# Sinkhorn-sorted attention and a gated MLP: one load for w_in, earlier loads for the next batch, a new order of units and a new last projection

## The chip, the cores and the metric

The kernel runs on one core of one Trainium2 chip. The metric is the device time of one execution in microseconds (us), the median of several runs. Data lies in device memory (DRAM), on chip in SBUF (128 partitions) and in PSUM, where TensorE's matmuls write. The engines work in parallel and wait for each other by semaphores: TensorE (PE in the profile, its weight loads PEld), VectorE (DVE), ScalarE (ACT), GpSimd (POOL) and SyncE (SP). DMAs are issued by POOL (these convert float32 to bf16 on the way) and by SP; the change adds one by ACT.

## The reference

Two layers follow each other. B = 4 batches, H = 8 heads, S = 768 positions, D = 64; a sequence has 8 blocks of 96 positions.

```python
# attention
P = sort_net                                    # (4, 8, 8, 8)
for _ in range(5):
    P = exp(P - max(P))
    P = P / sum(P, axis=-1)
    P = P / sum(P, axis=-2)
k_sorted = einsum('bhij,bhjcd->bhicd', P, k_b)  # mixes the blocks of a head
v_sorted = einsum('bhij,bhjcd->bhicd', P, v_b)
attn = softmax(q_b @ k_sorted^T / 8)            # inside each block of 96
x = (attn @ v_sorted) as (4, 768, 512)
# gated MLP
h = relu(x @ w_in)                              # 512 -> 1024
u, v = h[..., :512], h[..., 512:]
v_n = (v - mean(v)) / sqrt(var(v) + 1e-6)
v_s = einsum('ts,bsd->btd', w_spatial, v_n) + b_spatial
out = (u * v_s) @ w_out                         # float32 (4, 768, 512)
```

## The kernel before

Work is cut into *units*, each a short burst of matmuls on TensorE into one of four PSUM tiles (two banks each, `ps0` to `ps3`) and the copy, exp or relu that empties the tile. The order of the units, 174 of them, is written out by hand in `SCHEDULE` (lines 518 to 532). Line 538 makes PE, DVE, ACT and POOL follow the order of the program, so a unit's instructions stand on each engine's queue behind those of the unit before. `k10D3` reads: unit `k`, index 1, batch 0, emptied by DVE (`A` for ACT, `-` where the unit fixes it), into `ps3`. A unit can start on PE once its tile is empty and its operands are there.

The units of a batch, with their names in the schedule, are:

- `k` (line 321): the sorted k of two heads, transposed, by 12 matmuls against `pdiag`, the mixing matrix spread out for the layout. `q` (288): the transposed q of four heads, 24 matmuls.
- v comes in one of two ways. In batch 0, `t` (325) and `B` (328) mix and transpose it on PE. In later batches `v` (`vmix`, 261) mixes two heads with 2 matmuls; when both pairs of a half (four heads) are there, SP writes the half to a DRAM scratch `vd` (282) and reads it back as `vb` in another layout (283).
- `s` (`score`, 343): 16 matmuls of 96 x 96 and an exp on ACT into a tile `ex`. `z` (`sums`, 365): the softmax sums, and their reciprocals `lns` by two ACT instructions (375, 376). `a` (`attend`, 379): 32 small matmuls of `ex` with `vb`, four of them side by side in the array, and two DVE products (397) which write a quarter of `xt`, the transposed x.
- `X` and `V` (`vstart`, `vproj`, 427 to 444): the v half of `x @ w_in` in pieces of two row groups, relu on ACT, statistics on DVE. `N` (446) normalizes it. `U` (459): the u half, transposed.
- `S` (`spatial`, 472): `w_spatial` product, 12 matmuls, an add of the bias on DVE (490) and the gate product `gt` on POOL (491; in the last unit of all on DVE). `O` (`oproj`, 494): the product with `w_out`, 8 matmuls, a copy to `o_sb` and the DMA to the output, 512 KB for two row groups.
- `w` (228) transposes w_spatial once.

While the later half of batch b runs, the attention of batch b+1 is woven into it.

x is split so that one half of a head's 64 columns lies in one block of 128 partitions: `attend` takes columns 0 to 31 for `dh` = 0 and 32 to 63 for `dh` = 1 (line 390). The rows of w_in must lie in the same order, so it comes in four DMAs (lines 132 to 140), one for each half of the heads and of the columns.

Loads: `load_heads` (92) brings q, k or v of a batch as one DMA. POOL issues q, k and v of batch 0, w_in, the bias, w_spatial, then v, k and q of batch 1, and w_out; after them it makes `pdiag` of the later batches (547) and `b_bc` (549). The loads of batch b+2 are issued at line 565: after the second unit `S` of batch b, POOL copies two single elements of batch b+1's `vb` into a tile `gate`, which keeps POOL until that batch's v has come back from DRAM, and then issues v, k and q.

In the last batch every `O` unit empties its tile in pieces, DVE and ACT a half row group each, and sends each row group (256 KB) by itself (508 to 512).

Of the kernel before, what the change touches and what calls it, by code (L numbers as in the profile page):

```python
# [8 lines left out]
FP32 = mybir.dt.float32  # L9
BF16 = mybir.dt.bfloat16  # L10
# [6 lines left out]
def _raw_ap(base_ap: bass.AP, off_delta: int, dims) -> bass.AP:  # L17
    return bass.AP(
        tensor=base_ap.tensor,
        offset=base_ap.offset + off_delta,  # L20
        ap=[list(d) for d in dims],
    )
# [8 lines left out]
def kernel(  # L31
# [12 lines left out]
    nc = tc.nc  # L44

    B, H, S, D = q.shape
    NB = sort_net.shape[-1]
    BLK = S // NB
    G = S // 128
    TB = 128 // NB  # L50
    BH = B * H
    DM = H * D
    DFF = moe_w_in.shape[1]
    DH = DFF // 2
    KC = DM // 128
    FC = DH // 128
# [9 lines left out]
    qk_pool = ctx.enter_context(tc.tile_pool(name="qk", bufs=7))  # L66
    ex_pool = ctx.enter_context(tc.tile_pool(name="ex", bufs=8))
    xt_pool = ctx.enter_context(tc.tile_pool(name="xt", bufs=4))
    ln_pool = ctx.enter_context(tc.tile_pool(name="ln", bufs=4))
    moe_pool = ctx.enter_context(tc.tile_pool(name="moe", bufs=4))  # L70
    vs_pool = ctx.enter_context(tc.tile_pool(name="vs", bufs=3))
    vsb_pool = ctx.enter_context(tc.tile_pool(name="vsb", bufs=4))
# [6 lines left out]
    def ps_tile(n, dt=FP32):  # L79
        return psum.tile(  # L80
            [128, 2, 512 if dt == FP32 else 1024], dt, name=f"ps{n}", tag=f"ps{n}",
        )
# [9 lines left out]
    def load_heads(x, b, name):  # L92
        t = ld.tile([128, H, G * D], BF16, name=name, tag=name)
        nc.gpsimd.dma_start(  # L94
            out=t,
            in_=_raw_ap(x, b * H * S * D, [[G * D, 128], [S * D, H], [1, G * D]]),
        )
        return t
# [27 lines left out]
    DQ = D // 2  # L126
# [2 lines left out]

    v_in[0] = load_heads(v, 0, "v_in")  # L130
    w_in_sb = pers.tile([128, KC, DFF], BF16)
    for j in range(2):
        for dh in range(2):
            nc.gpsimd.dma_start(
                out=w_in_sb[:, 2 * j + dh, :],
                in_=_raw_ap(
                    moe_w_in, (j * (H // 2) * D + dh * DQ) * DFF,
                    [[D * DFF, H // 2], [DFF, DQ], [1, DFF]],
                ),
            )  # L140
    nc.gpsimd.dma_start(out=b_nat, in_=_raw_ap(moe_b_spatial, 0, [[0, 128], [1, S]]))
    wsp_nat = pers.tile([128, G, S], BF16)
    nc.gpsimd.dma_start(out=wsp_nat, in_=moe_w_spatial.rearrange("(p g) s -> p g s", g=G))
# [94 lines left out]
    def copy(eng, out, in_):  # L238
        if eng is nc.scalar:
            nc.scalar.copy(out=out, in_=in_)  # L240
        else:
            nc.vector.tensor_copy(out=out, in_=in_)  # L242
# [10 lines left out]
    class Attention:  # L253
# [126 lines left out]
        def attend(self, m, eng, ps):  # L380
            j, ih = m // 2, m % 2
            t = ps_tile(ps)
            for ii in range(NB // 2):
                i = ih * (NB // 2) + ii
                for dh in range(2):
                    for c in range(H // 2):
                        nc.tensor.matmul(  # L387
                            t[c * DQ:(c + 1) * DQ, dh, ii * BLK:(ii + 1) * BLK],
                            lhsT=self.vb[:, i, j, c, dh * DQ:(dh + 1) * DQ],
                            rhs=self.e[4 * j + 2 * (c // 2) + ih][:, c % 2, ii, :],  # L390
                            start=True, stop=True, tile_position=(0, c * DQ),
                        )
            if j not in self.xt:
                self.xt[j] = xts[self.b, j] = xt_pool.tile([128, 2, S], BF16, name="xt", tag="xt")
            i0, r = ih * (NB // 2), self.r[m]
            for dh in range(2):
                nc.vector.tensor_mul(  # L397
                    out=self.xt[j][:, dh, :].rearrange(
                        "p (g i t) -> p i g t", g=G, i=NB)[:, i0:i0 + NB // 2],
                    in0=t[:, dh, 0:HW].rearrange("p (i g t) -> p i g t", g=G, t=TB),  # L400
                    in1=r.rearrange("p (i g t) -> p i g t", g=G, t=TB),
                )


    class Gmlp:
        def __init__(self, b):
            self.b, self.last = b, b == B - 1
            self.v, self.u, self.gt, self.mv = {}, {}, {}, None
            self.vt = {}

        def xt(self, kc):
            return xts[self.b, kc // 2][:, kc % 2, :]
# [79 lines left out]
            self.gt[mc] = gt  # L492

        def oproj(self, n, eng, ps):
            t = ps_tile(ps)
            pairs = [(mc, x) for mc in range(FC) for x in range(2)]
            if self.last and n == G // 2 - 1:
                pairs = [(mc, x) for x in range(2) for mc in range(FC)]
            for mc, x in pairs:
                g = 2 * n + x  # L500
                nc.tensor.matmul(  # L501
                    t[:, x, :], lhsT=self.gt[mc][:, g * 128:(g + 1) * 128],
                    rhs=w_out_sb[:, mc, :],
                    start=(mc == 0), stop=(mc == FC - 1),
                )
            o_sb = o_pool.tile([128, 2, DM], FP32, name="o_sb", tag="o")
            o_dram = out[self.b].rearrange("(p g) n -> p g n", g=G)[:, 2 * n:2 * n + 2, :]
            if self.last:
                for x in range(2):
                    copy(DVE, o_sb[:, x, 0:DM // 2], t[:, x, 0:DM // 2])  # L510
                    copy(ACT, o_sb[:, x, DM // 2:], t[:, x, DM // 2:])
                    nc.sync.dma_start(out=o_dram[:, x, :], in_=o_sb[:, x, :])
            else:
                copy(eng, o_sb, t)
                nc.sync.dma_start(out=o_dram, in_=o_sb)


    SCHEDULE = """
        k00A2 k10D3 k20A0 s10-1 s00-2 s30-3 k30D0 t30D1 t00A2 t20D0 s20-3 s50-1 t10D2 s70-0
        B00D3 s60-1 s40-2 B30D0 B10D3 z00-1 B20D2 z10-0 a00-1 a10-3 z20-2 a20-0 z30-1 a30-2  # L520
        X10-3 X00-1 U20D0 V10-- V00-- w10D2 w30A0 V20-3 v01A1 U10A0 v11A3 v31D2 w00A1 U00D0
        k01A3 v21D1 w40A2 w20D0 w50D3 k11A1 k21A2 k31A0 q11D3 q01D1 N00-- U30A2 s51-0 s71-3
        S10-1 s31-2 s01-0 S20-3 s11-1 s21-2 S00-0 z31-3 z01-1 S30-2 s41-3 s61-0 a01-1 z11-2
        a31-3 a11-0 z21-1 a21-2 O10A3 O00D1 O20D0 V01-2 v32A3 v02D1 V21-0 v22A2 V11-3 v12A0
        U11A1 k32A2 q12D3 k12A0 q02D1 k02D2 N01-- k22A3 U21A0 s32-1 s22-3 S11-2 s72-0 s42-1
        S21-3 s52-2 s02-0 U01A1 s62-3 s12-2 U31D0 z02-1 S01-3 z32-2 z12-1 S31-0 z22-2 a32-3
        a02-1 a22-2 a12-0 O11D3 O01A1 O21A2 V02-0 v33A3 v03D1 V22-2 v23A0 V12-3 v13A2 U12A1
        k33A0 q13D3 k13A2 q03D1 k03D0 N02-- k23A3 U22A2 s33-1 s23-3 S12-0 s73-2 s43-1 S22-3
        s53-0 s03-2 U02A1 s63-3 s13-0 U32D2 z03-1 S02-3 z33-0 z13-1 S32-2 z23-0 a33-3 a03-1
        a23-0 a13-2 O12D3 O02A1 O22A0 V03-2 V13-3 V23-1 N03-- U03A0 U13A2 U23A3 U33A1 S03-0  # L530
        S13-2 S23-3 S33-1 O03A0 O13A2 O23A3
    """
    UNITS = {
        "v": "vmix", "k": "ktr", "q": "qtr", "s": "score", "z": "sums", "a": "attend",
# [3 lines left out]
    with tc.manual_schedule(engines={ET.PE, ET.DVE, ET.Activation, ET.Pool}):  # L538
        attn = {b: Attention(b) for b in range(B)}
        gmlp = {}  # L540
        sinkhorn()
        warm(9, 1)
        attn[0].qtr(0, ACT, 2), attn[0].qtr(1, ACT, 3)
        warm(2, 1)
        transpose_p()
        spread(0, 1, 0), spread(1, 3, 1)
        for x in range(1, B):
            make_pdiag(x, nc.gpsimd, 0, H)
        nc.gpsimd.tensor_copy(
            out=b_bc.rearrange("p (g c) -> p g c", g=G),  # L550
            in_=b_nat.rearrange("p (c g) -> p g c", g=G),
        )
        for step in SCHEDULE.split():
            name, n, b = step[0], int(step[1]), int(step[2])
            eng = {"A": ACT, "D": DVE, "-": None}[step[3]]
            ps = None if step[4] == "-" else int(step[4])
            if name == "w":
                wsp_unit(n, eng, ps)
            elif name in "XVNUSO":
                if b not in gmlp:  # L560
                    gmlp[b] = Gmlp(b)
                if name == "S":
                    eng = DVE if b == B - 1 and len(gmlp[b].gt) == FC - 1 else nc.gpsimd
                getattr(gmlp[b], UNITS[name])(n, eng, ps)
                if name == "S" and b + 2 < B and len(gmlp[b].gt) == 2:
                    gate = small.tile([1, 2], BF16, name="gate", tag="gate")
                    for x in range(2):
                        nc.gpsimd.tensor_copy(
                            out=gate[:, x:x + 1], in_=attn[b + 1].vb[0:1, 0, x, 0, 0:1],
                        )  # L570
                    v_in[b + 2] = load_heads(v, b + 2, "v_in")
                    k_in[b + 2] = load_heads(k, b + 2, "k_in")
                    q_in[b + 2] = load_heads(q, b + 2, "q_in")
            else:
                getattr(attn[b], UNITS[name])(n, eng, ps)


# [28 lines left out]
```

## Time and profile before

| | us |
|---|---|
| median of 8 runs | 166.55 (164.82 to 168.63) |
| the profiled execution, its own time | 165.71 |
| its span in the profile | 163.9 |
| PE busy with matmuls | 145.5 (89% of the span) |
| PE's weight loads | 85.4 |
| DVE busy | 98.7 |
| ACT busy | 92.2 |
| POOL busy | 50.4 |
| DMA traffic | 23.89 MB, 146 GB/s on average |

The chain of work that ended last is made of PE for 60% and of DMA for 19% of the span, the largest part of the latter being a load of q_in (11%). The granted clock of TensorE is 0.974 of full speed on average. A row of the profile's lists of waits gives the engine and line that waited, what ended the wait, the total in us, how often, and the longest. A row of a timeline gives the start in us, the duration of the (merged) instructions, engine and line, operation and operands; in brackets stands the idle time of the engine before it and what ended it.

### The profile page before, as it was taken

Reading aid. Unit: us, or ns where it says so; the run is one execution under the profiler, and the core shown is the slowest. Engines: PE = TensorE matmul, PEld = TensorE weight load, DVE = VectorE, ACT = ScalarE, POOL = GpSimd, SP = SyncE. Lnnn points to the kernel's source line nnn. Section 1 sums busy time; section 2 is a strip of 40 time slices with the busy share of each in tenths; the row PEclk is TensorE's granted clock in tenths of the full one; section 3 lists DMA queues with packets and bytes.
Section 4 is the critical chain, followed back from the end, with each engine's and each line's share of the span. In section 5 each row is a group of like instructions: output and inputs, shape, how many; then the busy total and the mean of one; then the engine's idle time right before and its main releaser. Section 6 shows DMA issues by size and latency. Waiting matters only on the chain.

```text
span 163.9 us, 4366 instructions
## 1 busy us (share of the span) xinstructions
PE 145.5 (89%) x1897; PEld 85.4 (52%) x1897; DVE 98.7 (60%) x201; ACT 92.2 (56%) x142; POOL 50.4 (31%) x52
## 2 busy tenths in 40 slices
PE   0958594999999999996999999999999999999970
PEld 0236583565775563444755554457655544556430
DVE  3776567439974474585942485399524763844751
ACT  3167596248787684177668633698776426570040
POOL 7942207940002694000037650000251600005600
PEclk9999779599999999999999999999999999999997
DMA  2999999999945369999720999947400018000055
GB/s 16 195 204 194 135 134 236 194 203 204 208 132 182 96 82 205 199 335 325 165 45 4 123 204 204 374 155 215 80 0 0 8 62 326 0 0 0 4 190 193
DMA packets 23139, 23.89 MB, mean 146 GB/s; under 512 B 2320, under 2 KB 19728, under 8 KB 22992
## 3 DMA queue, kind: packets, MB, share of 16 engines
q0 software_dynamic: 15344, 12.59, 51.8%
q1 hardware_dynamic: 7776, 11.02, 20.0%
q8 instruction: 15, 0.25, 0.6%
q14 instruction: 4, 0.03, 0.1%
HBM read 27.14 MB, written 8.65 MB: 218 GB/s over the span
## 4 chain that ended last, share of the span: by engine, by line
PE 60%; DMA 19%; DVE 8%; POOL 4%; issue 3%; ACT 2%; POOLq 1%; DVEq 0%
PE ps L479 16%; DMA q_in<-in_q_dram 11%; PE ps L463 11%; PE ps L501 9%; PE ps L420 9%; DMA v_in<-in_v_dram 8%; PE ps L350 4%; PE ps L307 4%; PE ps L295 3%; DVE stats L442 2%; PE ps L387 2%; PE ps L369 2%; DVE xt L397 1%; DVE vs L490 1%; POOL k_in L94 1%
## 5 line engine op out<-in xcount | busy, mean ns | idle before, releaser
L491 POOL TENSOR_TENSOR gt<-vs,u_sb 128x768 bf16<-128x768 f32 x15 | 24.6, 1644 | 88.6 <-ACT ex L357 61.3
L479 PE MATMUL ps<-wspT,v_sb 128*128 128x384 bf16 x192 | 33.4, 327 | 0.0
L490 DVE TENSOR_TENSOR vs<-ps,b_bc 128x768 f32<-128x768 f32 (+1 forms) x17 | 15.5, 910 | 21.7 <-PE ps L479 21.7
L357 ACT ACTIVATE ex<-ps 96x768 bf16<-96x768 f32 x32 | 24.0, 803 | 6.2 <-PE ps L350 6.1
L479 PEld LDWEIGHTS <-v_sb 128*128 128x128 bf16 x192 | 17.8, 98 | 12.5 <-issue 1.3
L420 PE MATMUL ps<-w_in_sb,xt 128*128 128x512 bf16 x96 | 23.6, 395 | 0.0
L442 DVE BATCH_NORM_STATS2 stats<-v_sb 128x6 f32<-128x512 bf16 x24 | 16.2, 675 | 11.4 <-ACT v_sb L246 11.4
L463 PE MATMUL ps<-xt,w_in_sb 128*128 128x384 bf16 x128 | 23.0, 327 | 0.0
L501 PE MATMUL ps<-w_out_sb,gt 128*128 128x512 bf16 x96 | 21.7, 379 | 1.3 <-DVE xt L397 0.8
L240 ACT COPY o_sb<-ps 128x256 f32<-128x256 f32 (+1 forms) x11 | 7.3, 663 | 23.9 <-PE ps L501 12.1
L246 ACT ACTIVATE v_sb<-ps 128x1024 bf16<-128x1024 f32 (+1 forms) x15 | 12.4, 852 | 14.4 <-PE ps L420 14.4
L397 DVE TENSOR_TENSOR xt<-ps,lns 128x384 bf16<-128x384 f32 x32 | 15.4, 549 | 1.6 <-PE ps L387 1.4
L463 PEld LDWEIGHTS <-w_in_sb 128*128 128x128 bf16 x128 | 11.9, 98 | 8.0
L501 PEld LDWEIGHTS <-gt 128*128 128x128 bf16 x96 | 8.9, 97 | 12.8 <-POOL gt L491 1.6
L420 PEld LDWEIGHTS <-xt 128*128 128x128 bf16 x96 | 9.6, 101 | 11.4 <-issue 1.7
L240 ACT CAST kT<-ps 128x768 bf16<-128x768 f32 x13 | 10.1, 800 | 5.3 <-PE ps L307 5.1
L375 ACT ACTIVATE lns<-ps 128x384 f32<-128x384 f32 x16 | 7.8, 485 | 6.5 <-PE ps L369 6.5
L246 ACT ACTIVATE u_sb<-ps 128x768 bf16<-128x768 f32 x12 | 9.5, 809 | 2.6 <-PE ps L463 2.3
L242 DVE COPY o_sb<-ps 128x256 f32<-128x256 f32 (+1 forms) x10 | 7.4, 742 | 4.8 <-PE ps L501 3.5
L387 PE MATMUL ps<-ex,vb 96*32 96x96 bf16 x512 | 7.9, 211 | 2.4 <-issue 2.3
L350 PEld LDWEIGHTS <-kT 64*96 64x96 bf16 x256 | 7.4, 127 | 4.6 <-issue 3.8
L350 PE MATMUL ps<-qT,kT 64*96 64x96 bf16 x256 | 9.6, 217 | 0.1
(74 smaller groups left out, 167.4 us busy)
## 6 DMA issues: line engine op xcount, KB each, us to landing
out_dram<-o_sb SPq DMA_DIRECT2D x9, 512.0 KB, 5.4
q_in<-in_q_dram POOLq DMA_DIRECT2D x4, 768.0 KB, 16.1
k_in<-in_k_dram POOLq DMA_DIRECT2D x4, 768.0 KB, 11.0
v_in<-in_v_dram POOLq DMA_DIRECT2D x4, 768.0 KB, 10.5
vd<-vm SPq DMA_DIRECT2D x6, 384.0 KB, 4.1
vb<-vd SPq DMA_DIRECT2D x6, 384.0 KB, 4.4
out_dram<-o_sb SPq DMA_DIRECT2D x6, 256.0 KB, 2.1
wsp_nat<-in_moe_w_spatial_dram POOLq DMA_DIRECT2D x1, 1152.0 KB, 22.9
```

The source lines that it names most:

```text
L240: nc.scalar.copy(out=out, in_=in_)
L246: nc.scalar.activation(out=out, in_=in_, func=AF.Relu)
L350: nc.tensor.matmul(t[0:BLK, hh, ii * BLK:(ii + 1) * BLK], lhsT=self.k[hp][rows, i * BLK:(i + 1) * BLK], rhs=self.q[hp][rows, i], start=Tru ...
L357: nc.scalar.activation(out=e.rearrange("p h i c -> p h (i c)"), in_=t[0:BLK, :, 0:NB // 2 * BLK], func=AF.Exp, scale=scale,)
L397: nc.vector.tensor_mul(out=self.xt[j][:, dh, :].rearrange("p (g i t) -> p i g t", g=G, i=NB)[:, i0:i0 + NB // 2], in0=t[:, dh, 0:HW].rearr ...
L420: nc.tensor.matmul(self.vt[n][:, x, :], lhsT=self.xt(kc)[:, g * 128:(g + 1) * 128], rhs=w_in_sb[:, kc, DH:DFF], start=(kc == 0), stop=(kc ...
L442: nc.vector.bn_stats(out=stats, in_=v_sb[:, x, :])
L463: nc.tensor.matmul(t[:, x, 0:HW], lhsT=w_in_sb[:, kc, mc * 128:(mc + 1) * 128], rhs=self.xt(kc)[:, x * HW:(x + 1) * HW], start=(kc == 0), ...
L479: nc.tensor.matmul(t[:, x, 0:HW], lhsT=self.v[g][:, mc * 128:(mc + 1) * 128], rhs=wspT[:, g, x * HW:(x + 1) * HW], start=(g == 0), stop=(g ...
L490: nc.vector.tensor_add(out=vs[:, x], in0=t[:, x, 0:HW], in1=b2[:, x])
L491: eng.tensor_mul(out=gt2[:, x], in0=vs[:, x], in1=u2[:, x])
L501: nc.tensor.matmul(t[:, x, :], lhsT=self.gt[mc][:, g * 128:(g + 1) * 128], rhs=w_out_sb[:, mc, :], start=(mc == 0), stop=(mc == FC - 1),)
```

## The change

- w_in is loaded by one DMA: a partition gets two neighbouring rows of each half. To match, `attend` takes the even columns d of a head for `dh` = 0 and the odd ones for `dh` = 1.
- The loads of batch b+1 are issued when the first score unit of batch b (1 or 2) has its exp, by a one-element copy on POOL of that exp's result. The loads behind the second `S` unit, with their gate on `vb`, are gone.
- The order of the units and their tiles and emptying engines are new; the set of units is the same.
- In the last batch, `O` units 0 and 1 are emptied whole, like those of the other batches. The last unit is computed in three parts on three PSUM tiles: row group 0, then the two column halves of row group 1. ACT copies the first two, DVE the third; the third's DMA is issued by ACT, the others by SP.
- The pool of `lns` has three buffers in place of four.

```diff
@@ pools
-    ln_pool = ctx.enter_context(tc.tile_pool(name="ln", bufs=4))
+    ln_pool = ctx.enter_context(tc.tile_pool(name="ln", bufs=3))
@@ w_in
-    for j in range(2):
-        for dh in range(2):
-            nc.gpsimd.dma_start(
-                out=w_in_sb[:, 2 * j + dh, :],
-                in_=_raw_ap(
-                    moe_w_in, (j * (H // 2) * D + dh * DQ) * DFF,
-                    [[D * DFF, H // 2], [DFF, DQ], [1, DFF]],
-                ),
-            )
+    nc.gpsimd.dma_start(
+        out=w_in_sb.rearrange("p (j x) f -> p j (x f)", x=2),
+        in_=moe_w_in.rearrange("(j p x) f -> p j (x f)", j=2, x=2),
+    )
@@ attend
-                            lhsT=self.vb[:, i, j, c, dh * DQ:(dh + 1) * DQ],
+                            lhsT=self.vb[:, i, j, c, :].rearrange("c (d x) -> c x d", x=2)[:, dh, :],
@@ oproj
+            self.ops.append(ps)
             t = ps_tile(ps)
+            o_dram = out[self.b].rearrange("(p g) n -> p g n", g=G)[:, 2 * n:2 * n + 2, :]
             if self.last and n == G // 2 - 1:
+                free = min(set(range(4)) - set(self.ops))
+                parts = ((0, 0, DM, t), (1, 0, DM // 2, ps_tile(free)), (1, DM // 2, DM // 2, None))
+                for x, c, width, tp in parts:
+                    tp = ps_tile(self.ops[0]) if tp is None else tp
+                    g = 2 * n + x
+                    for mc in range(FC):
+                        nc.tensor.matmul(
+                            tp[:, 0, 0:width], lhsT=self.gt[mc][:, g * 128:(g + 1) * 128],
+                            rhs=w_out_sb[:, mc, c:c + width],
+                            start=(mc == 0), stop=(mc == FC - 1),
+                        )
+                    o_x = o_pool.tile([128, width], FP32, name="o_x", tag=f"o{x}{c}", bufs=1)
+                    copy(DVE if c else ACT, o_x, tp[:, 0, 0:width])
+                    (nc.scalar if c else nc.sync).dma_start(
+                        out=o_dram[:, x, c:c + width], in_=o_x,
+                    )
+                return
...
-            if self.last:
-                for x in range(2):
-                    copy(DVE, o_sb[:, x, 0:DM // 2], t[:, x, 0:DM // 2])
-                    copy(ACT, o_sb[:, x, DM // 2:], t[:, x, DM // 2:])
-                    nc.sync.dma_start(out=o_dram[:, x, :], in_=o_sb[:, x, :])
-            else:
-                copy(eng, o_sb, t)
-                nc.sync.dma_start(out=o_dram, in_=o_sb)
+            copy(eng, o_sb, t)
+            nc.sync.dma_start(out=o_dram, in_=o_sb)
@@ SCHEDULE, the new one
+        k00A2 k10A3 k20D0 s10-1 s20-2 k30D3 s00-0 s30-1 t30D2 t10A3 t00D0 z10-1 t20D2 s40-3
+        B10D1 B00D0 z00-2 B30D3 s60-1 a10-2 a00-0 B20D3 s50-1 s70-2 z20-1 X10-0 z30-3 a20-2
+        a30-1 X00-3 V20-2 V10-- w30A1 V00-- U30A2 v11A0 v21A1 U20A3 w40D2 w10D0 N00-- U00A1
+        v01A3 U10A2 w20D0 w50D1 w00A3 k11D2 k31A0 q01D1 k01A3 q11A2 k21A0 v31A1 S00-3 s01-2
+        s11-0 S20-1 s51-3 s31-2 S10-0 z11-1 s21-3 S30-2 s61-1 a11-0 z01-3 a01-2 s71-1 s41-3
+        O10D0 z31-1 z21-2 O00A3 a31-1 a21-0 O20D2 V01-3 v12D1 v02A0 V11-2 v32A3 V21-0 v22A2
+        U01A1 k02A3 q12D0 k22A2 q02D1 k32A3 k12D0 U11D2 N01-- s42-1 s12-3 U21D0 s62-2 s02-1
+        S01-3 s32-2 s72-1 S11-0 s52-3 s22-2 S21-1 z02-0 z22-3 U31D2 z32-0 a32-1 S31-3 a22-2
+        z12-0 a12-1 a02-3 O21A0 O01D2 O11A1 V02-3 v13D0 v03A2 V12-1 v33A3 V22-2 v23A1 U02A0
+        k03A3 q13D2 k23A1 q03D0 k33A3 k13D2 U12D1 N02-- s43-0 s13-3 U22D2 s63-1 s03-0 S02-3
+        s33-1 s73-0 S12-2 s53-3 s23-1 S22-0 z03-2 z23-3 U32D1 z33-2 a33-0 S32-3 a23-1 z13-2
+        a13-0 a03-3 O22A2 O02D1 O12A0 V03-3 V13-2 V23-1 N03-- U03A0 U13A3 U23A2 U33A1 S03-0
+        S13-3 S23-2 S33-1 O03A0 O13A3 O23A2
@@ main loop
-                if name == "S" and b + 2 < B and len(gmlp[b].gt) == 2:
-                    gate = small.tile([1, 2], BF16, name="gate", tag="gate")
-                    for x in range(2):
-                        nc.gpsimd.tensor_copy(
-                            out=gate[:, x:x + 1], in_=attn[b + 1].vb[0:1, 0, x, 0, 0:1],
-                        )
-                    v_in[b + 2] = load_heads(v, b + 2, "v_in")
-                    k_in[b + 2] = load_heads(k, b + 2, "k_in")
-                    q_in[b + 2] = load_heads(q, b + 2, "q_in")
             else:
                 getattr(attn[b], UNITS[name])(n, eng, ps)
+                if name == "s" and 1 <= b < B - 1 and len(attn[b].e) == 1:
+                    gate = small.tile([1, 1], BF16, name="gate", tag="gate")
+                    nc.gpsimd.tensor_copy(out=gate, in_=attn[b].e[n][0:1, 0, 0, 0:1])
+                    v_in[b + 1] = load_heads(v, b + 1, "v_in")
+                    k_in[b + 1] = load_heads(k, b + 1, "k_in")
+                    q_in[b + 1] = load_heads(q, b + 1, "q_in")
```

More of the change, by code (lines that the diff above doesn't have):

```diff
@@ L408, in __init__ @@
             self.v, self.u, self.gt, self.mv = {}, {}, {}, None
-            self.vt = {}
+            self.vt, self.ops = {}, []
         def xt(self, kc):
@@ L494, in oproj @@
         def oproj(self, n, eng, ps):
+            self.ops.append(ps)
             t = ps_tile(ps)
-            pairs = [(mc, x) for mc in range(FC) for x in range(2)]
+            o_dram = out[self.b].rearrange("(p g) n -> p g n", g=G)[:, 2 * n:2 * n + 2, :]
             if self.last and n == G // 2 - 1:
[L498 to L504, printed above, removed]
-                )
@@ L506, in oproj @@
-            o_sb = o_pool.tile([128, 2, DM], FP32, name="o_sb", tag="o")
-            o_dram = out[self.b].rearrange("(p g) n -> p g n", g=G)[:, 2 * n:2 * n + 2, :]
-            if self.last:
-                for x in range(2):
-                    copy(DVE, o_sb[:, x, 0:DM // 2], t[:, x, 0:DM // 2])
-                    copy(ACT, o_sb[:, x, DM // 2:], t[:, x, DM // 2:])
-                    nc.sync.dma_start(out=o_dram[:, x, :], in_=o_sb[:, x, :])
-            else:
-                copy(eng, o_sb, t)
-                nc.sync.dma_start(out=o_dram, in_=o_sb)
@@ L518 @@
-    SCHEDULE = """
[L519 to L531, printed above, removed]
+                free = min(set(range(4)) - set(self.ops))
@@ new lines, in oproj @@
+                return
+            for mc in range(FC):
+                for x in range(2):
+                    g = 2 * n + x
+                    nc.tensor.matmul(
+                        t[:, x, :], lhsT=self.gt[mc][:, g * 128:(g + 1) * 128],
+                        rhs=w_out_sb[:, mc, :],
+                        start=(mc == 0), stop=(mc == FC - 1),
+                    )
+            o_sb = o_pool.tile([128, 2, DM], FP32, name="o_sb", tag="o")
+            copy(eng, o_sb, t)
+            nc.sync.dma_start(out=o_dram, in_=o_sb)
@@ L564 @@
                 getattr(gmlp[b], UNITS[name])(n, eng, ps)
-                if name == "S" and b + 2 < B and len(gmlp[b].gt) == 2:
-                    gate = small.tile([1, 2], BF16, name="gate", tag="gate")
-                    for x in range(2):
-                        nc.gpsimd.tensor_copy(
-                            out=gate[:, x:x + 1], in_=attn[b + 1].vb[0:1, 0, x, 0, 0:1],
-                        )
-                    v_in[b + 2] = load_heads(v, b + 2, "v_in")
-                    k_in[b + 2] = load_heads(k, b + 2, "k_in")
-                    q_in[b + 2] = load_heads(q, b + 2, "q_in")
             else:
                 getattr(attn[b], UNITS[name])(n, eng, ps)
+                if name == "s" and 1 <= b < B - 1 and len(attn[b].e) == 1:
[4 more added lines that the diff above has]
+                    q_in[b + 1] = load_heads(q, b + 1, "q_in")
 _INS = ['q', 'k', 'v', 'sort_net', 'moe_w_in', 'moe_w_spatial', 'moe_b_spatial', 'moe_w_out']
```

## The prediction

> **What bounds the kernel now.** I read the engine shares first, then the 40 slices, then TensorE's waits, then the timelines around each wait. TensorE (PE) is busy 145.5 of 163.9 us and the next engine, DVE, 98.7. Both schedules hold the same 174 units (counted by name, head pair and batch), so PE's matmul work stays. The change can only act on PE's 18.4 idle us, and on how fast PE is clocked.
>
> ```profile
> PE   0958594999999999996999999999999999999970
> ...
> PEclk9999779599999999999999999999999999999997
> DMA  2999999999945369999720999947400018000055
> ```
>
> A slice is 4.1 us. PE is filled from slice 7 on, but for slice 18 (the q load of batch 2) and the end. The clock is low in slices 4, 5 and 7; DMA is saturated from slice 1 to 10. The idle time before single matmuls is named by the waits:
>
> ```profile
> PE ps L387 <- issue: 2.3, 1, 2.3
> PE ps L307 <- DMA v_in<-in_v_dram: 2.2, 1, 2.2
> PE ps L295 <- DMA q_in<-in_q_dram: 1.9, 2, 1.5
> ...
> PE ps L501 <- DVE xt L397: 0.8, 2, 0.4
> PE ps L501 <- POOL gt L491: 0.3, 1, 0.3
> PE ps L369 <- DVE vs L490: 0.2, 1, 0.2
> ```
>
> The rest of PE's idle time is the front (3.9 us before the first matmul, 1.4 for the Sinkhorn chain, which the change leaves) and 4.9 us after the last matmul.
>
> **w_in as one DMA.** POOL's timeline shows what its DMAs wait for:
>
> ```profile
> 12.80 0.91 POOL L94 DMA_DIRECT2D v_in<-in_v_dram  x1 [2.61 <-DMA k_in<-in_k_dram]
> 18.39 0.88 POOL L94 DMA_DIRECT2D k_in<-in_k_dram  x1 [4.67 <-DMA v_in<-in_v_dram]
> 25.42 0.88 POOL L94 DMA_DIRECT2D q_in<-in_q_dram  x1 [6.16 <-DMA w_in_sb<-in_moe_w_in_dram]
> ```
>
> These are POOL's 10th, 11th and 12th DMA, and each waits for the landing of the 2nd, 3rd and 4th: at most eight in flight. With three DMAs fewer, v of batch 1 is the 7th and waits for nothing, q the 9th (waits for the first q, landed at 8.7), w_out the 10th (waits for 12.8). POOL issues one DMA of about 0.7 us in place of four (2.74), and the pdiag products of batches 1 to 3 (5.95 us from 27.06) can start near 14. None of this is on PE's path by itself: the loads go through the engines in order of issue and these are saturated until 41 us, so an earlier issue moves no landing. What moves landings is w_in's own rate: 136 to 137 GB/s from 16 to 24 us against 203 GB/s for the weight load behind it (33 to 37 us). 1.05 MB at 203 GB/s is 5.2 us, while w_in took from v's landing (18.1) to 24.3 at least, so wsp, v, k and q of batch 1 land 1 to 2 us earlier. They are needed later than that in this case, so I book 0; it matters in the first rival.
>
> **Even and odd d.** attend's stationary operand vb is now read with a step of two elements, in 512 weight loads. No row has that shape. The nearest is the transposed wsp_nat, read with a step of six: 125 ns for 128 columns against 98 ns for v_sb. Scaled to 32 columns that is 7 ns a load, 3.5 us in all if none were covered. The Trainium skill, "SBUF — State Buffer" (section "Door 1: The DMA port swizzle") says that accesses are free while at least two fall into one 16-byte line; a step of two puts four bf16 there, so the rule gives 0. The rows side with it: vb's loads (97 ns) lie beside 206 ns matmuls. I take 0, and keep 1 us for the range.
>
> **New order, first stage.** One more score unit (16 matmuls, 0.25 us: 0.49 for two) moves ahead of the wait for v_in (2.16 us), which shrinks by it. The larger hole is this one:
>
> ```profile
> 26.04 0.26 PE L387 MATMUL ps<-ex,vb 96*32 96x96 bf16 x6
> 28.59 0.48 PE L387 MATMUL ps<-ex,vb 96*32 96x96 bf16 x26 [2.29 <-issue]
> ```
>
> PE stops inside attend unit a20, after 6 of 32 matmuls, with all operands there: the seventh reads tiles that earlier ones read. It waits for instructions, I infer: the instruction queue moved 15 packets, 0.25 MB, in the span, about the size of PE's 3794 instructions. The Trainium skill, "Runtime: NRT & Kernel Launch" (section "Instruction fetch mechanics"), has blocks of 256 instructions fetched ahead, the crossing "mostly hidden". By that rule the hole is an accident worth nothing in a forecast and may go: 2.3 us, plus the clock (0.61 from 28.6 to 33: 0.39 x 4.4 = 1.7 us). By the row it comes back, since the new order issues the same number of instructions before this point (351 matmuls: now X10/z30) into the same saturated DMA. I take the row: it stays. Then, adding PE's durations from the hole to the first spatial product (X10 0.88, z 0.15, two attends 0.7, rest of X and V 4.4, clock 1.5, four U 5.6, six w 2, four v 1.3, four k 1.3, two q 1.3), S00 starts near 47.8; the same work stands at 48.3 now (48.31 in the chain). **Gain 0.5**, in which the score unit's 0.25 is contained. The early loads cover it: q of batch 1 is wanted near 45, and landed at 44.0.
>
> **Later loads.** The gate moves from the second gate product, and a wait for vb, to the first exp of each batch. Queued behind it on POOL are three issues (0.96+0.86+0.87 us) and then the next gate products, needed by the out projection over 6 us later. In batch 1 it follows the first product: S00's end + 0.97 + 1.64 + 0.2, so 5.0 us after unit v31. PE then reaches q12 25.7 us after v31: four S 8.24, eight s 2.0, z 0.6, four a 1.4, three O 5.2, three V 5.2, four v 1.3, U 1.41, k 0.33. That is 20.7 us after the issue; now q lands 19.8 us after its first issue (57.28 to 77.05). The wait of 1.9 us goes, with 0.9 to spare; as part of vb's traffic now lies beside the loads, I book **1.5** (bounds 0.9 and 1.9). For batch 3 the slack is about 8.
>
> **vb beside the loads.** Before, the gate kept the loads behind vb. Now vb's second half (vd out, vb back) runs beside them. PE needs it 15.0 us after v31 (the terms above as far as a31), in batch 2 16.9 after v22. The row: for batch 2 vd took 4.2 us with loads in flight (73 to 77), vb 5.3; with copies about 11 us. A rule of the Trainium skill speaks against the change: "DMA: Bandwidth & Descriptors" (section "Issuing engines are not separate DMA queues") says that all queues interleave on the same 16 engines. An even share would double the trip, to 20. By the row nothing is lost, by the rule up to 9 (below). I take the row, since it is the same neighbourhood.
>
> **Attend to out projection.** Waits of 1.3 us (0.8 xt, 0.3 gt, 0.2 vs) go, but the new order has its own: a01 sits on the bank of S30, whose add (0.97) ends 0.25 after PE arrives, O10 waits 0.2 for a11's xt; in batches 2 and 3 a0 comes 0.15 early and the last gt (1.0 + 1.64 after S3) about 0.2 late. 0.45 + 2 x 0.35 = 1.15. **Gain 0.1.** ln_pool loses a buffer: the fourth sum's Ln waits for an earlier attend. If it takes the oldest freed buffer, 0; if the newest, it waits for a22's xt and O21, on the same bank, 1.1 us, twice. I take 0 and keep 2.2 us for the range.
>
> **The tail.** After the last matmul (159.01) four copies run one after the other, each waiting for the one before:
>
> ```profile
> 159.03 0.42 DVE L242 COPY o_sb<-ps 128x256 f32<-128x256 f32 x1 [0.44 <-PE ps L501]
> 159.49 0.37 ACT L240 COPY o_sb<-ps 128x256 f32<-128x256 f32 x1 [0.49 <-DVE o_sb L242]
> 159.90 0.43 DVE L242 COPY o_sb<-ps 128x256 f32<-128x256 f32 x1 [0.44 <-ACT o_sb L240]
> 160.36 0.37 ACT L240 COPY o_sb<-ps 128x256 f32<-128x256 f32 x1 [0.49 <-DVE o_sb L242]
> ```
>
> They end at 160.73; 3.2 us follow. In the change x=0 is copied under the next matmuls (ACT, about 0.6 between 0.37 for 256 and 1.01 for 1024 columns), and the two halves of x=1 have banks and tiles of their own: what follows the last matmul is one DVE copy, 0.44, and an issue on ACT, free by then. 1.72 - 0.44: **gain 1.25**. O13's whole 512 KB leaves late, and 512 KB landed in 2.6 us at best against 2.1 for 256: issued 0.7 before PE's end it is there before the last piece, so 0.5 is the lower bound.
>
> **Sum.** 0.5 + 1.5 + 0.1 + 1.25 = 3.35 off the profiled execution's own 165.71 (span 163.9): 162.4. The median of the runs is 0.84 above that execution; off the median, 163.2, which I forecast.
>
> **Rivals.** (1) *The instruction hole goes* (chance 0.25). PE then runs ahead until the first loads of batch 1 stop it: q near 42.5 with w_in quicker, S00 at 44.8, a further 3.0: 160.2. For it: the rule, and fewer small packets in front of the fetch. Against: same instruction count, same full queues; w_in is now one large DMA. (2) *The new order stalls itself* (0.17): the ln buffer (2.2), the stride (1) or the new waits eat most of the gain: 165.5, from 164.5 to 166.5. For it: PE arrives within 0.2 us of several releases. (3) *vb takes the place of q_in* (0.11), the slower side. If loads double the round trip to 20.6 us, PE waits 5.6 at a31 and 3.7 at a32; 9.3 - 3.35 = 5.9 slower, 172.5. It decides from a trip of some 18 us on (3 + 1.1 waited). Against it is the 11 us row. (4) *The change doesn't bring the loads forward*, as POOL's gate still stands behind other work: the 1.5 are lost, 164.7; counted in (2).
>
> **Numbers.** Forecast 163.2 with 0.47; own range 162 to 164.5. 159.3 to 166.4 leaves out (3) and part of (1). What a measurement of this kernel can tell from no change is about 0.5%, 0.83 us. Faster by more: 0.47 + 0.25 + 0.1 of (2) = 0.82; within: 0.06; slower: 0.12.
>
> **What would show it.** Right: v, k, q of batch 1 issued before 12 us with no wait of PE for q_in; copies after the last matmul take 0.45 us; the issue hole near 26 us still there. Wrong: PE waiting for vb (L387 behind a DMA), for lns at O, or 60 ns more per vb load; a span above 164 means one of these.

## The result and the profile after

The changed kernel takes 0.960 of the time before (95% interval 0.956 to 0.964), 4.0% or 6.6 us of the 166.55. The medians of all its runs and all those of the kernel before, 158.78 and 167.44 us, lie further apart because each kernel also has slower runs, which the ratio leaves out. In the profiled executions the span falls from 163.9 to 157.4 us. PE's busy time is the same (144.9 us, before 145.5): what went is idle time.

The slices of the changed kernel's page, with PE's busy share, its clock and the DMA share in tenths:

```profile
PE   0958998999999999999999999999999999999970
...
PEclk9998589999999999999999999999999999999999
DMA  2999999999944999977699928248000054000054
```

Slice 7 is no longer low in clock, and slice 18 no longer low in work. (The low clock in slices 3 to 5 is this execution's own: in the experiments below with the same first stage the clock stays at 9 there.) All that the list of PE's waits has for the changed kernel:

```profile
PE ps L175 <- POOL ident_bf masks.py:199: 3.9, 1, 3.9
PE ps L206 <- DVE mask L149: 1.5, 1, 1.5
PE ps L290 <- DMA q_in<-in_q_dram: 0.8, 1, 0.8
PE ps L364 <- ACT ex L352: 0.5, 1, 0.5
PE ps L382 <- DVE vs L485: 0.5, 3, 0.2
```

The 2.3 us without a reason, the wait for v_in (2.2), that for q_in of batch 2 and the waits of the out projection are gone. The wait for q_in of batch 2 had been 1.45 us, in the kernel before:

```profile
77.07 0.86 PE L295 MATMUL ps<-ident_bf,q_in 128*64 128x128 bf16 x24 [1.45 <-DMA q_in<-in_q_dram]
```

The other 0.47 of the 1.9 us in its list was batch 0's at the very start, where the changed kernel waits 0.8. The chain of waits says the same: DMA had 19% of it.

```profile
PE 84%; DVE 8%; ACT 2%; POOLq 1%; issue 1%; DMA 1%; DVEq 0%
```

Cut at two points of PE's work, the 6.6 us of span (157.36 for 163.93) are:

| stretch | before, us | after, us | gained | forecast |
|---|---|---|---|---|
| start to the first spatial product (before: to the same work, 48.31) | 48.31 | 44.00 | 4.3 | 0.5 |
| from there to PE's last matmul | 110.7 | 108.33 | 2.4 | 1.5 + 0.1 |
| last matmul to the end of the span | 4.94 | 5.04 | -0.1 | 1.25 |

### The profile page after: what moved, and what is told of

The parts are those of the page before. It is cut to its first block, busy times and chain, and to the rows that moved or that the text cites. A ratio compares the mean times of both kernels' runs of the same rounds, so it can differ in the third digit from the quotient of the medians.

```text
span 157.4 us, 4345 instructions
## 1 busy us (share of the span) xinstructions
PE 144.9 (92%) x1901; PEld 85.7 (54%) x1901; DVE 98.0 (62%) x197; ACT 92.7 (59%) x139; POOL 48.4 (31%) x47
## 4 chain that ended last, share of the span: by engine, by line
PE 84%; DVE 8%; ACT 2%; POOLq 1%; issue 1%; DMA 1%; DVEq 0%
PE ps L474 19%; PE ps L458 14%; PE ps L415 13%; PE ps L515 12%; PE ps L302 5%; PE ps L345 5%; PE ps L382 3%; PE ps L290 3%; PE ps L260 3%; DVE vs L485 2%; PE ps L364 2%; PE ps L329 1%; PE ps L226 1%; PE ps L501 1%; POOLq L605 1%
## 5 line engine op out<-in xcount | busy, mean ns | idle before, releaser
L415 PE MATMUL ps<-w_in_sb,xt 128*128 128x512 bf16 x96 | 22.4, 380 | 0.0
L515 PE MATMUL ps<-w_out_sb,gt 128*128 128x512 bf16 x88 | 20.2, 380 | 0.1
L235 ACT COPY o_sb<-ps 128x1024 f32<-128x1024 f32 x7 | 7.1, 1013 | 18.0 <-PE ps L515 18.0
L415 PEld LDWEIGHTS <-xt 128*128 128x128 bf16 x96 | 9.1, 98 | 10.6 <-DVE xt L392 0.4
L515 PEld LDWEIGHTS <-gt 128*128 128x128 bf16 x88 | 7.9, 98 | 10.2 <-POOL gt L486 1.2
L345 PE MATMUL ps<-qT,kT 64*96 64x96 bf16 x256 | 10.6, 222 | 0.1
L235 ACT CAST kT<-ps 128x768 bf16<-128x768 f32 x12 | 9.3, 800 | 1.7 <-PE ps L302 1.7
L237 DVE CAST kT<-ps 128x768 bf16<-128x768 f32 x8 | 7.6, 955 | 2.9 <-PE ps L302 2.8
L448 DVE TENSOR_SCALAR v_sb<-v_sb,mv,rstd 128x512 bf16<-128x512 bf16 x24 | 8.3, 418 | 0.6 <-ACT rstd L446 0.6
L371 ACT ACTIVATE lns<-lns 128x384 f32<-128x384 f32 x16 | 8.4, 523 | 0.5
```

The costliest lines, as they stand in the source:

```text
L345: nc.tensor.matmul(t[0:BLK, hh, ii * BLK:(ii + 1) * BLK], lhsT=self.k[hp][rows, i * BLK:(i + 1) * BLK], rhs=self.q[hp][rows, i], start=Tru ...
L415: nc.tensor.matmul(self.vt[n][:, x, :], lhsT=self.xt(kc)[:, g * 128:(g + 1) * 128], rhs=w_in_sb[:, kc, DH:DFF], start=(kc == 0), stop=(kc ...
L515: nc.tensor.matmul(t[:, x, :], lhsT=self.gt[mc][:, g * 128:(g + 1) * 128], rhs=w_out_sb[:, mc, :], start=(mc == 0), stop=(mc == FC - 1),)
```

## The experiments

Each ratio is to the kernel before, run on the same chip, with its 95% interval. The kernel before took 166.71 us beside e1 to e4 and 166.97 beside e5 to e8 (medians), so a difference of a few tenths of a per cent between two ratios means little.

**e1: w_in alone.** The kernel before, with the w_in load and the matching attend operand of the change:

```diff
-                    [[D * DFF, H // 2], [DFF, DQ], [1, DFF]],
...
+        in_=moe_w_in.rearrange("(j p x) f -> p j (x f)", j=2, x=2),
...
-    lhsT=self.vb[:, i, j, c, dh * DQ:(dh + 1) * DQ],
+    lhsT=self.vb[:, i, j, c, :].rearrange("c (d x) -> c x d", x=2)[:, dh, :],
```

> The kernel before with w_in as one DMA of row pairs and the even/odd split of x, nothing else. Theory W (PE's hole of 2.3 us near 26 us is a refill of its instructions that queues behind w_in's small packets): the hole goes, w_in's stretch from 16 to 24 us runs at over 200 GB/s, the clock stays up, and PE reaches its first spatial product 3 to 4 us earlier; the wait for q_in stays, so 3 to 4 us faster, some 163.5 beside 167. Rival O (the new order removes the hole): hole and time stay, within 1 us of before. If the weight loads with a step of two cost anything, attend's 512 loads get longer than 97 ns.

Measured: 0.972 (0.962 to 0.983), from few runs. PE reaches its first spatial product at 45.25 us and not 48.73, 3.5 us earlier. The traffic summary of the page, first of the kernel before, then of e1:

```profile
DMA packets 23139, 23.89 MB, mean 146 GB/s; under 512 B 2320, under 2 KB 19728, under 8 KB 22992
```

```profile
DMA packets 21299, 23.88 MB, mean 149 GB/s; under 512 B 736, under 2 KB 18144, under 8 KB 21152
```

The same bytes, with 1584 fewer packets under 512 B, and from 16 to 24 us the DMA engines move 238 GB/s in place of 137. So w_in's old form had cost DMA rate, and not its own time alone: v of batch 0, ahead of it, lands sooner too (PE's wait for v_in falls from 2.16 to 0.35 us). The gain fits theory W within its interval, but its reason is only half right, as the hole is still there. PE's timeline of e1 at that place:

```profile
25.30 0.74 PE L382 MATMUL ps<-ex,vb 96*32 96x96 bf16 x26 [1.72 <-issue]
```

attend's weight loads with a step of two take 97 ns at the median, as before.

**e2: the order alone.** The kernel before with the new `SCHEDULE`, nothing else.

> The kernel before with the new order of units alone; w_in in four DMAs, old loads, old tail. Theory W: the hole stays, or is as long at another unit (the 351st matmul), and the refill lands near 26 us as before; gain at most 1 us. Rival O: the hole goes, 3 to 4 us faster. Under both the wait for q_in of batch 2 stays, 1 to 3 us, as the loads still follow the second spatial product and the gate on vb, which now comes later.

Measured: 1.000 (0.996 to 1.004). Against theory W, PE's hole is gone, as rival O expected, and the first spatial product starts at 45.74 us, 3.0 earlier. But nothing of it is left at the end. PE's waits in e2, of its list:

```profile
PE ps L501 <- POOL gt L491: 2.5, 2, 1.9
PE ps L307 <- DMA v_in<-in_v_dram: 1.7, 1, 1.7
PE ps L295 <- DMA q_in<-in_q_dram: 1.6, 3, 0.9
```

The first row is new: the out projection waits for the gate products on POOL. After it PE's clock is low as well (0.72 from 62 to 68 us). The reason stands in e8.

**e5: the early loads alone.** The kernel before with the loads of batches 2 and 3 behind the first exp:

```diff
-                if name == "S" and b + 2 < B and len(gmlp[b].gt) == 2:
...
+                if name == "s" and 1 <= b < B - 1 and len(attn[b].e) == 1:
...
```

> The kernel before with the loads of batches 2 and 3 behind the first exp of the batch, nothing else. My step: the wait for q_in (1.9 us) goes, vb still comes in time: 1.5 to 2 us faster. Rival (vb takes its place): PE waits at an attend unit behind vb, as much or more than is gained.

Measured: 1.009 (1.003 to 1.015), slower. The wait for q_in did shrink (1.9 to 0.4 us, the rest being batch 0's). Two losses stand against it in the attention of batch 1, beside the loads now in flight. PE's weight loads and matmuls there:

```profile
62.12 0.72 PEld L387 LDWEIGHTS <-vb 96*32 96x32 bf16 x64 [1.59 <-DMA vb<-vd]
```

```profile
62.12 0.86 PE L387 MATMUL ps<-ex,vb 96*32 96x96 bf16 x64 [1.35 <-ACT lns L376]
62.81 0.34 PE L369 MATMUL ps<-ex,ones 96*32 96x384 bf16 x4
62.97 0.50 PE L387 MATMUL ps<-ex,vb 96*32 96x96 bf16 x29
64.66 0.22 PE L387 MATMUL ps<-ex,vb 96*32 96x96 bf16 x3 [1.19 <-issue]
```

The first loss, 1.35 us, is vb, as the rival expected. The matmuls' row names the reciprocals on ACT, which end at the same moment, but an attend's matmuls do not read them (its DVE products do), and the row of the weight loads names vb. SP issued vb's second half at 52.68; its landing, 9.4 us later, falls on 62.1, when unit a31 starts, which reads it:

```profile
vb<-vd SPq DMA_DIRECT2D x1, 384.0 KB, 9.4
```

In the kernel before, where the gate on POOL kept the loads behind vb, the same DMA took 3.8 us. The second loss is a hole of the kind seen at 26 us, 1.19 us in the middle of unit a21. After these PE's clock is low (0.81 from 66 to 72 us) during the out projection, which takes 6.9 us there and 5.5 in the kernel before. The first hole is longer as well (3.9 us), but lies before any early load (the first is issued at 51.28): PE only came to it sooner, as v_in of batch 0 held it up less (1.0 us).

**Where the holes lie.** Counting PE's matmuls from the start, and finding the packet of the instruction queue (queue 8 of the DMA table) nearest before:

| kernel | stops after weight load | in unit | refill packet at, us | PE goes on at, us | stopped, us |
|---|---|---|---|---|---|
| before | 351 | a20 | 26.25 | 28.59 | 2.3 |
| e1 | 351 | a20 | 22.88 | 25.30 | 1.7 |
| e5 | 351 | a20 | 25.98 | 28.31 | 3.9 |
| e5 | 862 | a21 | 62.14 | 64.66 | 1.2 |
| e2 | 351 | z30 | 25.39 | 27.67 | 0.2, weight loads alone |
| after | none | (z30) | 23.44 | (reached at 27.23) | |

Three kernels stop behind the same matmul, and the second stop comes 511 later; with a weight load each that is 1022 instructions, four of the prediction's blocks of 256 within two. PE goes on 2.3 to 2.5 us after the packet. The new order puts another unit at that count and so tests the count itself: the 352nd weight load is then the third of four in z30. In e2 it starts 0.22 us after the second, and 2.28 us after the packet; in the changed kernel, where the packet was 3.8 us old, the four follow each other at once. Their rows, of e2 and of the changed kernel:

```profile
27.44 0.32 PEld L369 LDWEIGHTS <-ones 96*32 96x32 bf16 x4 [0.42 <-issue]
```

```profile
27.23 0.10 PEld L364 LDWEIGHTS <-ones 96*32 96x32 bf16 x4 [0.42 <-issue]
```

In e2 a matmul of 0.34 us covers the pause, so PE's own rows show no hole. The stop thus belongs to the count and the packet, and not to the unit: PE waits for a block of its instructions. With the old order PE has run through short attend instructions by then, and is there at the packet in the kernel before and 0.7 us after it in e1. In the new order B20, two score units and X10, four wide matmuls, stand between the first two attends and that point, and PE arrives 2.1 us (e2) and 3.8 us (after) behind the packet. What sets the time of the packet itself was not tested.

**e8: the old gate in the changed kernel.** The loads go back behind the second `S` unit and the copies of two elements of vb.

> The changed kernel with the loads back behind the second spatial product and the gate on vb. If the early loads are what took q_in's wait away: PE waits again for q_in of batch 2, 2 to 4 us slower (the gate waits for vb, which is now finished later in the order). If the new order took it away: within 0.5 us.

Measured: 0.979 (0.974 to 0.984) of before, so 1.9% of before, 3.2 us, slower than the changed kernel (3.7 us by the medians of e8 and of e6, run beside it, which is the changed kernel but for its tail). POOL's timeline of e8:

```profile
50.78 0.18 POOL L575 COPY gate<-vb 1x1 bf16<-1x1 bf16 x1
52.70 0.18 POOL L575 COPY gate<-vb 1x1 bf16<-1x1 bf16 x1 [1.74 <-DMA vb<-vd]
53.20 0.96 POOL L94 DMA_DIRECT2D v_in<-in_v_dram  x1 [0.32 <-issue]
...
55.91 3.27 POOL L486 TENSOR_TENSOR gt<-vs,u_sb 128x768 bf16<-128x768 f32 x2
```

and what PE does of it:

```profile
55.37 0.39 PE L515 MATMUL ps<-w_out_sb,gt 128*128 128x512 bf16 x1
57.64 1.04 PE L515 MATMUL ps<-w_out_sb,gt 128*128 128x512 bf16 x4 [1.88 <-POOL gt L486]
59.23 0.67 PE L515 MATMUL ps<-w_out_sb,gt 128*128 128x512 bf16 x2 [0.56 <-POOL gt L486]
```

The new order finishes vb's second half later, so the old gate holds POOL for 1.74 us (0.54 in the kernel before); with three load issues behind it (2.7 us), the third and fourth gate products start at 55.91, when PE already stands at the out projection. In the changed kernel they run from 51.74. After the two waits PE's clock is low too, 0.75 from 60 to 66 us, where the changed kernel has 1.00. This is also e2's loss, with a gate held for 2.01 us. PE's waits for q_in come to 1.4 us in three places, but only 0.8 of it, in batch 3, is due to the loads; in batch 2, where the expectation looked for it, there is none.

**e3 and e4: four DMAs for w_in in the changed kernel.** e3 kept the grouping of the kernel before in the code, e4 wrote the rows as one dimension of 128 (the last two lines, in this order, are the rows of a DMA in e3 and in e4):

```diff
-        in_=moe_w_in.rearrange("(j p x) f -> p j (x f)", j=2, x=2),
...
+                    moe_w_in, (j * (H // 2) * D + dh) * DFF,
+                    [[D * DFF, H // 2], [2 * DFF, DQ], [1, DFF]],
...
+                    [[2 * DFF, 128], [1, DFF]],
```

> The changed kernel with w_in back in four DMAs, each with rows in four groups of 32 as before (but every second row, for the even/odd layout). Theory W: the small packets are back (over 2000 under 512 B in the page in place of 720), the hole too, 3 to 4 us slower than the changed kernel, some 162.5. Rival O: as the changed kernel, 159.

> The changed kernel with w_in in four DMAs, each over 128 rows in one dimension (every second row, 4 KB read). It has the number of DMAs and the waits of POOL of the kernel before, but not its grouping. Theory W with the small packets as the cause: few packets under 512 B, no hole, time within 0.5 us of the changed kernel. Rival L (the number of DMAs and POOL's waits for places in flight matter): the hole is back, 3 us slower, and v, k, q of batch 1 land later than they are wanted.

Measured: 0.956 (0.949 to 0.963) and 0.954 (0.946 to 0.962), as the changed kernel. Both pages show 769 packets under 512 B: with every second row, 32 rows of step two fill exactly one group's distance, so e3's groups join into one dimension and it is the same load as e4. e3 therefore failed as a test of the small packets. Together they show that the number of DMAs is not what costs (rival L falls), and point to the old form, four groups of 32 rows that do not join. Under the new order that form still costs: e2 has it and e8 does not, both with the old loads. Up to the first spatial product they differ in little else (the operand of attend and the pool of `lns`), and they reach it at 45.74 and 43.47 us; as a whole they take 1.000 and 0.979 of before, though e8 has the new tail as well. Under the early loads it was not tried.

**e6 and e7: the tail.** e6 puts the old last projection into the changed kernel; e7 splits O unit 1 of the last batch:

```diff
+            if self.last and n == 1:
+                for x, e in ((0, DVE), (1, ACT)):
+                    o_sb = o_pool.tile([128, 2, DM], FP32, name="o_sb", tag="o")
+                    copy(e, o_sb[:, 0, :], t[:, x, :])
+                    nc.sync.dma_start(out=o_dram[:, x, :], in_=o_sb[:, 0, :])
+                return
             copy(eng, o_sb, t)
```

> The changed kernel with the last batch's out projection as before. My forecast of the tail (1.25 us for shorter copies): 1.25 us slower than the changed kernel. Rival (the end is set by the 1 MB that still has to go out after PE's last matmul, at some 400 GB/s): within 0.4 us of the changed kernel; from PE's last matmul to the end of the span 4.9 us here and 5.1 there.

> The changed kernel with O unit 1 of the last batch emptied by DVE and ACT side by side, a row group each, and sent as two DMAs of 256 KB. If the end is set by output bytes that leave late: they start some 0.4 us earlier and the kernel ends 0.3 to 0.5 us earlier, 158.4. If it is set by the last copy and the latency of its DMA: no difference.

Measured: e6 0.957 (0.952 to 0.961), no slower than the changed kernel; e7 0.951 (0.946 to 0.956), the lowest of all, with an interval that just touches the changed kernel's. From PE's last matmul to the end of the span it is 5.3 us in e6, 4.8 in e7, 5.0 in the changed kernel, but 4.6 to 4.7 in e3, e4 and e8, which have the same tail. The new tail does what was forecast up to the last issue:

```profile
151.67 0.33 SPq L522 DMA_DIRECT2D out_dram<-o_sb  x1
152.15 1.14 SPq L508 DMA_DIRECT2D out_dram<-o_x  x2
152.36 0.42 DVE L237 COPY o_x<-ps 128x256 f32<-128x256 f32 x1 [3.11 <-PE ps L501]
152.82 0.38 ACTq L508 DMA_DIRECT2D out_dram<-o_x  x1
```

One copy of 0.42 us follows the last matmul. Then the DMA engines' rate from 148 to 157.4 us, in 40 slices of 0.235 us:

```profile
GB/s 0 0 0 0 0 0 0 0 0 0 0 122 418 418 401 418 401 53 0 401 401 418 383 453 270 375 401 331 340 340 318 31 0 0 0 0 0 0 0 35
```

From slice 19 (152.5 us) to 31 (155.5) they move data without a pause, at 270 to 450 GB/s: the whole 512 KB of O13, issued at 151.67, and the three last pieces, 1 MB. The last issue waits its turn.

The traces separate the tails better than the run times. From PE's last matmul to the end of the last output packet it is 3.43 us in all five traces with the old tail (before, e1, e2, e5, e6), 3.06 to 3.08 in the four with the new one (the changed kernel, e3, e4, e8) and 2.84 in e7. What follows, up to the end of the span, is 1.5 to 1.6 us in seven traces and 1.9 to 2.0 in three (the changed kernel, e6, e7), with old and new tails in both groups; its cause stays open. So the new tail is worth 0.4 us, and the -0.1 in the table is the longer ending of that one execution. In e6 the last 256 KB are issued at 154.24 and done 1.67 us later, so there the chain of copies still sets the end; in the changed kernel the last 128 KB take 2.58 us from their issue, behind the other bytes. e7's further 0.2 us fits 256 KB that leave earlier; by the times alone (medians of 158.39 and 158.67) it is not separated from nothing.

**vb, found on the way.** In the profiles of e4, e6 and e7 PE waits 1.1 to 1.4 us for vb at the first attend of batch 1; e6's timeline:

```profile
54.42 0.53 PE L382 MATMUL ps<-ex,vb 96*32 96x96 bf16 x32 [1.07 <-DMA vb<-vd]
```

vb's first half was there by 47.9 (issued 44.45, 3.4 us), the second lands at 54.3 (issued 48.80, 5.5 us beside the loads). a11 reads the first half, and goes on when the second has landed. In the changed kernel's own profile the second half takes 4.0 us, and PE, slowed by its clock at the start, comes later: no wait. In e3 PE is the earliest of all and does not wait either, as the trip took 4.1 us. With e5's 9.4, the same DMA beside the loads took 4.0 to 9.4 us; it took at most 3.9 in the kernel before, e1, e2 and e8, which issue the loads behind it.

## Why the prediction was right and where it failed

Faster was right. Set against the median shown before, 0.960 of 166.55 is 159.9: inside the outer range (159.3 to 166.4), but below the 162 to 164.5 of the likeliest case, which had half of the gain, 3.35 us for 6.6. That case has the mechanism of the first stage and the size of the tail wrong; what came true there is the first rival, given a chance of 0.25. The direction was reasoned, but that the total stayed in the outer range is in part luck, as errors of both signs met in it.

- **The first stage** (0.5 forecast, 4.3 found). The step that failed is "By the row it comes back, since the new order issues the same number of instructions before this point ... I take the row: it stays." The place was right, 351 matmuls. What decides, though, is when PE gets there against when the refill lands: PE comes 0.9 us later (27.2 for 26.3), the packet 2.8 earlier. e2 shows the order alone to be enough for the hole to go (0.2 us is left, hidden under a matmul), e1 that w_in alone leaves 1.7 us of it. (A score unit has 8 matmuls, not the 16 that the prediction gives it; its 0.25 us is right.) So the first rival's time came true (160.2 forecast). The Trainium skill's "mostly hidden" ("Runtime: NRT & Kernel Launch", section "Instruction fetch mechanics") describes the new order, in which no more than 0.2 us shows; the row described the old one.
- **w_in** was booked at 0, because loads "are needed later than that in this case". The rate gain was named (203 for 136 GB/s) but taken to start behind w_in only; v of batch 0, whose wait of 2.2 us was on PE's path, also gained: the forecast took 0.25 us off that wait, e1 takes 1.8. Alone w_in is worth 2.8%.
- **The later loads** (1.5 forecast): the wait in batch 2 is gone, and e8 shows that without the early loads the kernel loses 3.2 us. But the term met its size by luck: the 1.9 us read as one wait were two, 1.45 in batch 2 and 0.47 in batch 0, and most of e8's loss is not q_in but the gate on POOL, 2.4 us of waits for gate products. That PE could be short of instructions beside the early loads was not priced; e5, with the old order, has such a hole of 1.2 us, and no run with the new order has one. That the loads held its packet up is likely, but was not tested.
- **vb beside the loads**: 0 was taken, and 0 is in the changed kernel's profile. But the step "By the row nothing is lost" does not hold in general: the third rival is there in e5 (1.35 us), e4, e6 and e7 (1.1 to 1.4), if far from 9.3. The slack was wrong too: not a31, 15 us after v31, is the deadline but a11, some 10 us after, since it goes on only with both halves landed.
- **Attend to out projection** (0.1 forecast): PE's idle time after the first spatial product falls from 3.1 to 0.7 us; without q's 1.45 that is 1.0. PE waits nowhere for `lns`, and the loads with a step of two take 97 ns at the median as before.
- **The tail** (1.25 forecast, with 0.5 as lower bound; 0.4 found by the packets). The term mis-sized is "issued 0.7 before PE's end it is there before the last piece". O13's DMA was issued 0.66 before PE's end, but its data and the pieces behind it keep the engines full for 3.0 us. The copies did get shorter by what was forecast; the bytes then set the end.

## What to carry to other kernels

When an engine stops in the middle of a unit with nothing to wait for, count its instructions from the start: if the stop keeps its count when other units stand there, it is the instruction feed. Here it was hidden where wide matmuls ahead of that count brought the engine there 2.1 us or more after the refill's packet; w_in's better form alone only shortened it. When a wait has an odd name, look at the weight loads' row and at the landings near its end: in e5 two things ended together, and the list named the wrong one. Parts of a change are worth what they are worth together: the order alone gained nothing, the early loads alone lost 0.9% and w_in alone gained 2.8%, yet all of them gained 4.0%, and taking the early loads out again cost 1.9%. For a tail, add up the bytes that still have to leave after the last matmul before shortening the copies.

## What was unexpected of the hardware

- PE's weight loads resumed 2.3 to 2.5 us after the start of the refill packet in all five stops, whether the stop lasted 0.2 or 3.9 us.
- A load whose 128 rows come as four groups of 32 that do not join brought some 1600 packets under 512 B; from 16 to 24 us the engines moved 137 GB/s with it and 238 GB/s with row pairs (e1).
- The same read of 384 KB from a DRAM scratch, vb's second half, took at most 3.9 us with the next batch's loads held behind it, and 4.0 to 9.4 us beside them.
